# Two banks of one PSUM tile treated as one: the waits between them declared unneeded in a fused attention and gated-product kernel

## The chip, the core and the metric

The kernel runs on one core of a Trainium2 chip. A core has a matrix engine (PE, with weight loads listed apart as PEld), a vector engine (DVE), a scalar engine (ACT), a general engine (POOL), and a sequencer (SP) that issues the transfers which 16 DMA engines carry out. The engines run on their own and wait for each other by semaphores. The matrix engine writes its results into PSUM, which has eight banks; ACT and DVE read them from there.

The metric is the device time of one execution in microseconds (us). A profile adds the span between the first and the last instruction of one execution, which is a little shorter than the device time.

## What is computed

A recurrent attention with a forget gate runs over 768 steps for 4 batches and 8 heads of width 48. Its result, 3072 tokens of width 384, goes through a gated product of inner width 2048.

```python
# q, k, v, f_logit: (4, 8, 768, 48)
f = 1.0 / (1.0 + np.exp(-f_logit))
for t in range(S):
    state = f[:, :, t, :, None] * state + np.einsum('bhd,bhe->bhde', k[:, :, t], v[:, :, t])
    y[:, :, t] = np.einsum('bhd,bhde->bhe', q[:, :, t], state)
x = y.transpose(0, 2, 1, 3).reshape(B * S, H * D)   # (3072, 384)
h = x @ w_in                                        # (3072, 2048)
g = h * np.cos(h)
out = g @ w_out                                     # (3072, 384)
```

The kernel works in chunks of 128 steps. Within a chunk, scores of queries against keys are masked and multiplied with the values; across chunks a small state per head is carried (`st`, `sz` in the profile). The chunk's result `xT` has its channels on the partitions, so that the gated product can use it directly.

## The kernel before

A planner written in Python places every operation on an engine, gives it its buffers and fixes the order; the operations are then emitted in that order, and the framework adds the semaphores by looking at which tiles each instruction reads and writes.

PSUM is handed out from four tiles that are two banks wide each. A large operation takes a whole tile; a small one takes one bank, that is, one half of a tile.

```python
def halves(name, n, width, dt, space=None, zero=None):
    ts = [(space or cpool).tile([128, 2 * width], dt, name=f"{name}_{i}") for i in range(n)]
    # ... (cut)

base = halves("ps", 4, 512, F32, space=ppool)          # 4 tiles of two banks
phS = Banks(base, 2, [0, 2, 4], "ph")                   # h = x @ w_in: whole tiles
scS = Banks(base, 2, [4, 6, 2], "sc")                   # scores and others: whole tiles
p1S = Banks(base, 1, [7, 6, 5, 4, 3, 2, 1, 0], "p1")    # one bank

# class Banks (cut)
def ap(self, s):
    t, w = self.base["tiles"][s // 2], self.base["width"]
    return t if self.size == 2 else t[:, (s % 2) * w:(s % 2) * w + w]
```

The gated product works on units of 128 or 256 tokens. First h into two banks (line 728), its cosine on ACT (line 735), and the product of the two on DVE (line 738), which gives the tile gT:

```python
nc.tensor.matmul(ph.ap[:, g * T:(g + 1) * T], lhsT=w_in_bf[...], rhs=x[:, m, :], ...)   # L728
# ACT: co = sin(h + pi/2)                                                                # L735
# DVE: gT = h * co                                                                       # L738
```

Then the output product, 16 matmuls for each 128 tokens into one bank, planned as four operations of four so that other work can stand between them, and a copy out of PSUM (on ACT or DVE) that is then stored:

```python
for i in range(T // C):
    po, ot = Val(p1S), Val(otS)
    for s in range(4):
        def g2(e, i=i, s=s, po=po):
            for j in range(4 * s, 4 * s + 4):
                nc.tensor.matmul(po.ap[:, 0:d_model], lhsT=gT.ap[:, j, i * C:(i + 1) * C],
                                 rhs=w_out_bf[:, j, :], start=(j == 0), stop=(j == KF - 1))   # L748
        P.op("o", {"PE": mm(384, 4)}, g2, reads=[gT, w_out_v[s]], writes=[po], prio=pr)
    P.op("ot", {"ACT": act(384), "DVE": dve(384)}, ...)                                       # L751
    # the store of ot, L759 and L762 (cut)
```

The attention of one chunk, as far as its lines are named further on:

```python
# qk: queries and keys times decay, on POOL or DVE          L540, L632
# vb, vz: values cast to bf16, on ACT, POOL or DVE           L403
# qkt: queries and keys turned, by PE (L559, L654) and a copy out of PSUM (L427), or by DMA (L645)
# sc: scores, PE                                             L572, L667
# am: scores times mask, DVE                                 L578, L670
# ps: the chunk's own part of the state, PE                  L592, L680
# st: that part + the state before, DVE                      L497
# sz: st times decay, POOL (in the first chunk DVE)          L504
# px: the chunk's result, PE                                 L705 (first chunks: L611, L618)
# xT: its copy out of PSUM, ACT or DVE                       L427
# cum: sums of the gate's logarithm, PE                      L465 to L477
```

Of the kernel before, what the change touches and what calls it, by code (L numbers as in the profile page):

```python
# [15 lines left out]
class Slots:  # L16


    def __init__(self, aps, name):
        self.aps, self.name = aps, name  # L20
        self.free_at = [0.0] * len(aps)
        self.held = [False] * len(aps)
        self.last, self.now = [[] for _ in aps], [[] for _ in aps]
# [87 lines left out]

class Op:
    __slots__ = ("seq", "eng", "fn", "prio", "table", "deps", "vals", "alloc", "start", "end",
                 "lat", "waiting", "after", "grp", "dma", "name", "prior", "cost")


class Plan:
# [126 lines left out]
        return order  # L244


GROUPS = [(2, 2), (2, 2), (2, 2), (2, 2), (2, 2), (2, 2)]
UNITS = [128, 128] + [256] * 11
DUAL = [0, 2, 4]
# [29 lines left out]
       "DVE", 759: "ACT", 775: "ACT", 776: "ACT", 778: "DVE", 782: "ACT", 803: "ACT", 809: "ACT"}  # L279


def build(nc, cpool, ppool, q, k, v, f_logit, moe_w_in, moe_w_out, out):
    B, H, S, D = 4, 8, 768, 48
    C = 128
    NCH = S // C
# [45 lines left out]
    def halves(name, n, width, dt, space=None, zero=None):  # L331
        ts = [(space or cpool).tile([128, 2 * width], dt, name=f"{name}_{i}") for i in range(n)]
        if zero is not None and nc is not None:
            for t in ts:
                zero(t)
        return {"held": [False] * 2 * n, "free": [0.0] * 2 * n, "last": [[] for _ in range(2 * n)],
                "now": [[] for _ in range(2 * n)], "tiles": ts, "width": width}
# [25 lines left out]
    base = halves("ps", 4, 512, F32, space=ppool)  # L363
# [1 line left out]
    scS = Banks(base, 2, [4, 6, 2], "sc")  # L365
    p1S = Banks(base, 1, [7, 6, 5, 4, 3, 2, 1, 0], "p1")

    P = Plan()
    HB = lambda a: a.rearrange("p (h d) -> p h d", d=D)

    def act(n, src="P", ptr=False):
        return 0.833 * n + (160 if src == "P" else 198) + (95 if ptr else 0) - 55

# [11 lines left out]
    def load_weights(part, i, prio):  # L385
# [6 lines left out]
        def fn(e):  # L392
            if part == 0:
                src = moe_w_in.rearrange("(km p) f -> p km f", p=128)[:, :, i * 512:(i + 1) * 512]
            else:
                src = moe_w_out.rearrange("(kf p) m -> p kf m", p=128)[:, i * 4:(i + 1) * 4, :]
            nc.sync.dma_start(out=view(), in_=src)
        P.op(f"w{part}{i}", {"SP": 420.0}, fn, writes=[stage], prio=prio, dma=2080.0)
        P.op("wc", {"POOL": 1480.0, "DVE": 920.0, "ACT": act(1536, "S")}, lambda e:
             cast(e, dst.ap, view()), reads=[stage], writes=[dst], prio=PR["wc"][4 * part + i])  # L400

    def cast(e, o, i_):
        (nc.scalar.copy if e == "ACT" else nc.vector.tensor_copy if e == "DVE" else nc.gpsimd.tensor_copy)(  # L403
            out=o, in_=i_)

    def load(t, src, b, c, n, prio, nm, eng="SP"):

        def fn(e):
# [3 lines left out]
            else:  # L412
                i_.dma_start(out=o.rearrange("p (h x) -> p h x", h=H),
                             in_=src[b, :, c * C:(c + 2) * C, :].rearrange("h (p e) d -> p h (e d)", e=2))
        P.op(nm + str(n), {eng: 430.0 if n not in DUAL else 500.0}, fn, writes=[t], prio=prio,
             dma=1000.0 if n not in DUAL else 1430.0)
# [12 lines left out]
    def decay(chunks, g, prio):  # L429
# [5 lines left out]
        for i, (b, c, n) in enumerate(chunks[:1] if dual else chunks):  # L435
            load(ft.part((lambda a: flat(a)) if dual else (lambda a, i=i: a[:, i].rearrange("p h d -> p (h d)"))),
                 f_logit, b, c, n, PR["f"][n], "f")

        first = P.op("exp", {"ACT": act(384 * m, "S")}, lambda e: nc.scalar.activation(  # L439
            out=flat(ft.ap[:, 0:m]), in_=flat(ft.ap[:, 0:m]), func=AF.Exp, scale=-1.0),  # L440
# [329 lines left out]
    n, t0, units = 0, 0, list(UNITS)  # L770
    for g, group in enumerate(GROUPS):
        at0 = n
# [23 lines left out]
@with_exitstack  # L796
def kernel(
    ctx: ExitStack,
    tc: tile.TileContext,
    q: bass.AP,  # L800
    k: bass.AP,
    v: bass.AP,
    f_logit: bass.AP,
    moe_w_in: bass.AP,
    moe_w_out: bass.AP,
    out: bass.AP,
):
    nc = tc.nc
    cpool = ctx.enter_context(tc.tile_pool(name="const", bufs=1))
    ppool = ctx.enter_context(tc.tile_pool(name="psum", bufs=1, space=bass.MemoryType.PSUM))  # L810
    with tc.manual_schedule():
        order = build(nc, cpool, ppool, q, k, v, f_logit, moe_w_in, moe_w_out, out).run()
        table = None
        for o in order:
            if o.table is not None:
                if o.table == "E" and table != "E":
                    nc.scalar.preload_act_table_set("natural_log_exp_and_others")
                table = o.table
            o.fn(o.eng)


# [28 lines left out]
```

## Time and profile before

| | |
|---|---|
| device time, median of 3 runs | 202.4 us (202.11 to 203.04) |
| span in the profile | 199.2 us |
| L748, output product | 384 matmuls, 69.7 us busy, 326 ns each |
| L728, product h | 624 matmuls, 68.5 us busy |
| L738, DVE product of h and cosine | 48, 58.1 us busy, 1220 ns each |
| L735, ACT cosine | 48, 53.3 us busy, 1115 ns each |
| L751, copy of the output | 14 on ACT, 482 ns each; 10 on DVE, 557 ns each |

In the profile, PE, DVE and the others are rows of instructions, each with its source line. An idle time in front of an instruction is put down to the releaser, the instruction whose semaphore came last. Idle time of an engine costs something only where the chain of work that ends last runs through that engine. A wait in front of an instruction can have two reasons: it needs what the other has made, or the other still uses the place into which it will write. The view does not say which of the two it is; that is read from the source.

### The profile page before, as it was taken

The page shows a single profiled execution, that of the slowest core. Times are in us where ns is not written, and L with a number is a line of the kernel's source. Part 1 is how long each engine was busy: PE and PEld are TensorE (multiplying, and loading weights), DVE is VectorE, ACT ScalarE, POOL GpSimd, SP SyncE. Part 2 cuts the span into 40 slices and gives each one's busy share as a digit, 9 for nine tenths or more (in the row PEclk, how much of TensorE's full clock was granted, in tenths as well). Part 3 has the DMA queues.
Part 4 walks back from the last instruction along what each step waited for, and adds up shares of the span by engine and source line. Part 5 has one row for each costly group of instructions (what it writes and reads, how often), then busy time and mean ns, then how long its engine had stood idle before and what let it go on. Part 6 is the DMA issues. An engine that isn't in the chain of part 4 may idle for free. (4 is left out here: it accounts for less than half of the span.)

```text
span 199.2 us, 5276 instructions
## 1 busy us (share of the span) xinstructions
PE 176.3 (89%) x2194; PEld 129.0 (65%) x2194; DVE 123.8 (62%) x152; ACT 130.7 (66%) x163; POOL 75.7 (38%) x119
## 2 busy tenths in 40 slices
PE   0477999999999988998999999998998899998883
PEld 0355898765678755767866678755776657885451
DVE  5139689838868931786991778973474694587100
ACT  3694578987668978987789658878564454572010
POOL 8337232139631108879523972127902220000000
PEclk9999999999999999999999999999999999999999
DMA  6999999999899799799999999951331210101212
GB/s 158 302 277 313 358 252 294 207 298 236 171 191 214 168 204 220 174 220 186 192 216 174 242 216 179 216 120 44 94 95 40 53 44 3 40 0 40 81 40 79
DMA packets 106264, 33.11 MB, mean 166 GB/s; under 512 B 99584, under 2 KB 104704, under 8 KB 106240
## 3 DMA queue, kind: packets, MB, share of 16 engines
q1 hardware_dynamic: 106240, 32.78, 74.9%
q8 instruction: 17, 0.28, 0.7%
q14 instruction: 7, 0.06, 0.1%
HBM read 25.17 MB, written 4.72 MB: 150 GB/s over the span
## 5 line engine op out<-in xcount | busy, mean ns | idle before, releaser
L748 PE MATMUL ps<-w_out_bf,gT 128*128 128x384 bf16 x384 | 69.7, 326 | 7.0 <-DVE ot L751 2.6
L735 ACT ACTIVATE cosh<-ps,halfpi 128x1024 bf16<-128x1024 f32 x48 | 53.3, 1115 | 23.8 <-PE ps L728 23.1
L728 PE MATMUL ps<-xT,w_in_bf 128*128 128x256 bf16 (+1 forms) x624 | 68.5, 267 | 0.4
L738 DVE TENSOR_TENSOR gT<-ps,cosh 128x1024 bf16<-128x1024 f32 x48 | 58.1, 1220 | 15.1 <-ACT cosh L735 12.8
L728 PEld LDWEIGHTS <-w_in_bf 128*128 128x128 bf16 x624 | 57.1, 99 | 8.6 <-DVE xT L427 0.5
L748 PEld LDWEIGHTS <-gT 128*128 128x128 bf16 x384 | 35.5, 97 | 31.1 <-issue 9.2
L504 POOL TENSOR_TENSOR sz<-st,b 64x192 bf16<-64x192 f32 x32 | 16.3, 510 | 31.0 <-DVE st L497 29.7
L632 POOL TENSOR_TENSOR qk<-ld,b 128x384 bf16<-128x384 f32 x18 | 18.5, 1044 | 14.4 <-ACT b L483 9.1
L670 DVE TENSOR_TENSOR am<-ps,umask 128x1024 bf16<-128x1024 f32 x18 | 21.9, 1218 | 3.1 <-PE ps L667 2.8
L751 ACT COPY ot<-ps 128x384 f32<-128x384 f32 x14 | 6.7, 482 | 18.3 <-PE ps L748 17.2
L632 POOL TENSOR_TENSOR qk<-ld,bi 128x384 bf16<-128x384 f32 x18 | 17.8, 1002 | 0.2
L403 POOL CAST vb<-ld 128x384 bf16<-128x384 f32 x13 | 6.6, 507 | 25.7 <-DMA ld<-in_v_dram 19.8
L497 DVE TENSOR_TENSOR st<-ps,sz 128x384 f32<-128x384 f32 x16 | 8.8, 552 | 8.8 <-PE ps L748 5.9
L751 DVE COPY ot<-ps 128x384 f32<-128x384 f32 x10 | 5.6, 557 | 12.8 <-PE ps L748 10.2
L483 ACT ACTIVATE b<-ps 128x776 f32<-128x776 f32 x12 | 9.8, 820 | 5.5 <-PE ps L471 2.3
L439 ACT ACTIVATE f<-f 128x768 f32<-128x768 f32 x12 | 9.7, 840 | 3.6 <-DMA f<-in_f_logit_dram 3.5
L483 ACT ACTIVATE bi<-ps 128x768 f32<-128x768 f32 x12 | 9.8, 814 | 0.0
L454 ACT ACTIVATE sp<-f 128x768 bf16<-128x768 f32 x12 | 9.5, 829 | 0.1
L427 DVE COPY qkt<-ps 128x1024 bf16<-128x1024 bf16 x8 | 5.5, 687 | 6.0 <-ACT vz L403 2.0
L559 PE MATMUL ps<-ident,qk 128*128 128x128 bf16 x48 | 5.5, 279 | 3.5 <-DVE qk L540 2.2
L578 DVE TENSOR_TENSOR am<-ps,pmask 128x1024 bf16<-128x1024 f32 x6 | 7.2, 1221 | 1.9 <-PE ps L572 1.9
L465 PE MATMUL ps<-sp,incl 128*128 128x384 bf16 x6 | 2.6, 431 | 6.3 <-ACT sp L454 6.3
(77 smaller groups left out, 182.4 us busy)
## 6 DMA issues: line engine op xcount, KB each, us to landing
f<-in_f_logit_dram SPq DMA_DIRECT2D x18, 192.0 KB, 3.7
ld<-in_v_dram SPq DMA_DIRECT2D x18, 192.0 KB, 4.0
ld<-in_k_dram SPq DMA_DIRECT2D x18, 192.0 KB, 3.8
ld<-in_q_dram SPq DMA_DIRECT2D x18, 192.0 KB, 3.6
out_dram<-ot SPq DMA_DIRECT2D x18, 192.0 KB, 1.9
gT<-in_moe_w_in_dram SPq DMA_DIRECT2D x4, 768.0 KB, 7.6
gT<-in_moe_w_out_dram SPq DMA_DIRECT2D x4, 768.0 KB, 7.4
f<-in_f_logit_dram SPq DMA_DIRECT2D x3, 384.0 KB, 6.0
```

The lines of the kernel that those rows point to most:

```text
L439: first = P.op("exp", {"ACT": act(384 * m, "S")}, lambda e: nc.scalar.activation(out=flat(ft.ap[:, 0:m]), in_=flat(ft.ap[:, 0:m]), func=AF ...
L454: nc.scalar.activation(out=o, in_=i_, func=AF.Ln, bias=1.0)
L483: nc.scalar.activation(out=out_.ap[:, 0:m, :], in_=i, func=AF.Exp, scale=s)
L497: P.op("st", {"DVE": dve(384)}, lambda e: nc.vector.tensor_add(out=like(st.ap, pv()), in0=pv(), in1=like(S_in.ap, pv())), reads=[ps[0], S_ ...
L504: eng().tensor_mul(out=like(S_out.ap, pv())[s, ..., r, :], in0=srcap()[s, ..., r, :], in1=d[..., None].broadcast_to(list(d.shape) + [D]))
L632: P.op("qk", {"POOL": 1020.0}, lambda e, j=j, src=src, dec=dec: E(e).tensor_mul(out=qkv()[:, j, :, 0:D], in0=HB(src.ap), in1=HB(dec.ap[:, ...
L670: P.op("am", {"DVE": dve(1024)}, lambda e: nc.vector.tensor_mul(out=am.ap.rearrange("p r a n -> p (r a) n"), in0=sc.ap.rearrange("p (a n) ...
L728: nc.tensor.matmul(ph.ap[:, g * T:(g + 1) * T], lhsT=w_in_bf[:, f0 // 512, m, f0 % 512:f0 % 512 + 128], rhs=x[:, m, :], start=(g % (G // 2 ...
L735: nc.scalar.activation(out=co.ap, in_=ph.ap, func=AF.Sin, bias=halfpi),
L738: P.op("g", {"DVE": dve(1024)}, lambda e, ph=ph, co=co, gv=gv: nc.vector.tensor_mul(out=gv.ap, in0=ph.ap.rearrange("p (g t) -> p g t", t=T ...
L748: nc.tensor.matmul(po.ap[:, 0:d_model], lhsT=gT.ap[:, j, i * C:(i + 1) * C], rhs=w_out_bf[:, j, :], start=(j == 0), stop=(j == KF - 1))
L751: P.op("ot", {"ACT": act(384), "DVE": dve(384)}, lambda e, po=po, ot=ot: (nc.scalar.copy if e == "ACT" else nc.vector.tensor_copy)(out=ot. ...
```

## The change

The framework tracks who reads and who writes each PSUM tile. In the kernel before, the two banks of a tile are one thing to it: an instruction that writes into one bank waits for the readers of the other, and a reader of one bank waits for the writers of the other, though no byte is shared. The change records every emitted instruction and tells the framework, for each operation that uses PSUM, that it has no dependence on operations of other engines in the other bank of its tile. Dependences that the plan itself knows of (what an operation reads, and who used its buffers before) are kept. Order and instructions are those of before, and so are the places in PSUM.

```diff
+def apart(tc, o, base):
+    banks = set()
+    for v in o.vals:
+        if getattr(v.pool, "base", None) is base:
+            banks.update(range(v.slot, v.slot + v.pool.size))
+    others = [b ^ 1 for b in sorted(banks) if b ^ 1 not in banks]
+    keep = [i for d in list(o.deps) + o.prior for i in d.made]
+    for b in others:
+        for e in ("PE", "ACT", "DVE", "POOL"):
+            if e != o.eng:
+                for i in o.made:
+                    tc.declare_no_dep(i, group=f"bank{b}{e}", keep=keep, reason="other PSUM bank")
+    if banks and len(others) == len(banks):
+        for b in banks:
+            for i in o.made:
+                tc.add_to_no_dep_group(f"bank{b}{o.eng}", i)
 ...
-        order = build(nc, cpool, ppool, q, k, v, f_logit, moe_w_in, moe_w_out, out).run()
+        rec = Recorded(nc)
+        P = build(nc, cpool, ppool, q, k, v, f_logit, moe_w_in, moe_w_out, out, rec)
+        order = P.run()
         ...
+            del rec.made[:]
             o.fn(o.eng)
+            o.made = list(rec.made)
+            apart(tc, o, P.banks)
```

Cut here: the classes `Recorder` and `Recorded`, which pass each call on to the engine and keep the instruction that it returns, and a field `made` for it. An operation that uses a whole tile (both banks) declares nothing and joins no group.

More of the change, by code (lines that the diff above doesn't have):

```diff
@@ L113 @@
     __slots__ = ("seq", "eng", "fn", "prio", "table", "deps", "vals", "alloc", "start", "end",
-                 "lat", "waiting", "after", "grp", "dma", "name", "prior", "cost")
+                 "lat", "waiting", "after", "grp", "dma", "name", "prior", "cost", "made")
 class Plan:
@@ L244, in run, with __init__, __getattr__, call @@
         return order
+class Recorder:
+    def __init__(self, engine, to):
+        self._engine, self._to = engine, to
+    def __getattr__(self, name):
+        f = getattr(self._engine, name)
+        def call(*a, **k):
+            r = f(*a, **k)
+            self._to.append(r.ins)
+            return r
+        return call
+class Recorded:
+    def __init__(self, nc):
+        self.made = []
+        for e in ("tensor", "vector", "scalar", "gpsimd", "sync"):
+            setattr(self, e, Recorder(getattr(nc, e), self.made))
+def apart(tc, o, base):
[14 more added lines that the diff above has]
+                tc.add_to_no_dep_group(f"bank{b}{o.eng}", i)
 GROUPS = [(2, 2), (2, 2), (2, 2), (2, 2), (2, 2), (2, 2)]
@@ L279, with build @@
        "DVE", 759: "ACT", 775: "ACT", 776: "ACT", 778: "DVE", 782: "ACT", 803: "ACT", 809: "ACT"}
-def build(nc, cpool, ppool, q, k, v, f_logit, moe_w_in, moe_w_out, out):
+def build(nc, cpool, ppool, q, k, v, f_logit, moe_w_in, moe_w_out, out, rec=None):
     B, H, S, D = 4, 8, 768, 48
@@ L366, in build @@
     p1S = Banks(base, 1, [7, 6, 5, 4, 3, 2, 1, 0], "p1")
-    P = Plan()
+    P, nc = Plan(), rec or nc
+    P.banks = base
     HB = lambda a: a.rearrange("p (h d) -> p h d", d=D)
```

## The prediction

> **What bounds the kernel now.** I read the page's first two parts, then the waits of the matrix engine (PE) by stage, then the timeline around its gaps.
>
> ```profile
> PE 176.3 (89%) x2194; PEld 129.0 (65%) x2194; DVE 123.8 (62%) x152; ACT 130.7 (66%) x163; POOL 75.7 (38%) x119
> ...
> PE   0477999999999988998999999998998899998883
> ...
> DMA  6999999999899799799999999951331210101212
> ```
>
> The first line is busy time and share by engine, the other two are busy tenths in slices of 5 us. PE works nearly without a break from 20 us to 195 us, so what takes idle time out of PE can shorten the kernel. The DMA line shows a second thing that is full: the 16 DMA engines, until about 127 us (slice 25). After that DMA hardly matters. By stage (the table of windows) the DMA share is 0.96 from 50 to 97.6 us and 0.86 from 97.6 to 150 us, and 0.13 after.
>
> Next, who makes PE idle. Columns: engine, line, releaser, total us, times, longest. First 50 to 97.6 us, then 97.6 us to the end.
>
> ```profile
> PE ps L748 <- DVE ot L751: 1.3, 2, 0.6
> PE ps L680 <- ACT xT L427: 0.6, 1, 0.6
> ```
>
> ```profile
> PE ps L748 <- DVE ot L751: 1.3, 2, 0.6
> PE ps L748 <- DVE xT L427: 1.1, 2, 0.6
> PE ps L748 <- DVE qkt L427: 0.8, 1, 0.8
> PE ps L748 <- ACT ot L751: 0.8, 2, 0.6
> PE ps L748 <- ACT xT L427: 0.6, 1, 0.6
> PE ps L748 <- DVE st L497: 0.4, 1, 0.4
> ```
>
> In the second stretch all of PE's idle time of note, 5.0 us in nine waits, stands before the output product (L748). A matmul there needs only the gated tile, the weights and a bank of PSUM. None of the named releasers makes any of these: ot, xT, qkt and st are copies or sums that read PSUM, so PE waits until someone has finished reading. The timeline shows what they read:
>
> ```profile
> 179.59 1.46 PE L748 MATMUL ps<-w_out_bf,gT 128*128 128x384 bf16 x8
> ...
> 181.09 0.56 DVE L751 COPY ot<-ps 128x384 f32<-128x384 f32 x1 [0.24 <-PE ps L748]
> ...
> 181.70 5.36 PE L748 MATMUL ps<-w_out_bf,gT 128*128 128x384 bf16 x32 [0.65 <-DVE ot L751]
> ```
>
> Eight matmuls: the last four of one accumulation and the first four of the next, which stands in the other bank of the same two-bank tile. The copy needs only the first four, which end at 180.40 us (179.59 + 3 x 0.162 + 0.326, pitch and length from below), yet it starts at 181.09, after all eight. Then PE waits for the copy, 0.56 us and the hand-over, before it goes on in the bank that the copy never touches. It is a wait in each direction, and neither carries data.
>
> **What the Trainium skill says.** "PSUM — Partial Sum Buffer", section "PSUM bank collisions raise a hardware error", reports that two engines on different banks run clean, so the order that is given up here protects nothing. The trace agrees as far as it goes: the copy of ot takes 0.56 us at 181.09 with PE idle and 0.56 us at 183.85 in the midst of matmuls into another tile. "Perfetto Trace Analysis", section "Identifying the Most-Contended Engine", warns that pipelined matmuls make busy time a poor measure. That matters for the sum: 32 matmuls of 326 ns take 5.36 us, so their pitch is (5.36 - 0.33)/31 = 0.162 us, and a gap in a row of them costs its idle time plus the lost overlap, 0.326 - 0.162 = 0.16 us. Section "Identifying Dependency Chains" of the same page says that an instruction waiting on several engines may get an extra semaphore instruction. One such on PE shows in the trace, 51 ns long.
>
> **The change part by part.** *Removed.* In the built program 27 matmuls lose a wait for ACT or DVE or get it later, and 22 reads of PSUM by ACT and DVE wait for an earlier matmul than before. Matching each lost wait with the gap in front of it, after 97.6 us: 109.87 us 0.39, 130.45 us 0.48, 137.39 us 0.65, 151.05 us 0.83, 156.48 us 0.57, 162.38 us 0.24, 181.70 us 0.65, 187.71 us 0.65, 193.63 us 0.57. The sum is 5.03 us: every one of the nine goes. Six of them stand between two matmuls of L748 (all but those at 109.87, 130.45 and 162.38), so 6 x 0.16 = 0.98 us of overlap comes back: 6.0 us.
>
> *Before 97.6 us* the lost waits measure 0.28, 0.18, 0.32 (all at 51 to 56 us), 0.65 (71.61 us) and 0.65 (78.67 us), with the overlap some 2.9 us, and part of 0.63 at 94.64 us. I choose to count almost none, because the loads do not come sooner:
>
> ```profile
> 91.31 0.51 ACT L403 CAST vb<-ld 128x384 bf16<-128x384 f32 x1 [1.47 <-DMA ld<-in_v_dram]
> ...
> 92.10 2.12 ACT L735 ACTIVATE cosh<-ps,halfpi 128x1024 bf16<-128x1024 f32 x2
> ...
> 93.25 2.36 DVE L738 TENSOR_TENSOR gT<-ps,cosh 128x1024 bf16<-128x1024 f32 x2 [1.41 <-ACT cosh L735]
> ...
> 94.11 0.49 ACT L427 CAST xT<-ps 128x384 bf16<-128x384 f32 x1
> ...
> 94.64 0.33 PE L680 MATMUL ps<-vb,qk 128*128 128x96 bf16 x4 [0.63 <-ACT xT L427]
> ```
>
> ACT sits at a cast until its load lands at 91.29 us, in a stream that fills the DMA engines, and then works without a gap through a cast, a copy and two cosines to the xT copy that ends at 94.60. L680 no longer has to wait for that copy, but the L728 matmul after it reads that xT, and may start at 94.64 instead of 94.81. DVE follows the same load: its row of five operations from 93.25 ends at 97.49, and frees the tile for the L728 matmul that now starts at 97.60. So PE can be ahead by no more than about 0.06 us at 97.6, however much it gained before. I add 0.1 us.
>
> *Added.* Nine semaphore instructions, three on ACT and six on DVE, none on PE; at 51 ns, under 0.5 us spread over two engines with a third of their time free. *Moved.* Order and instructions stay.
>
> *What stays behind it.* A gain is real only if the next wait does not catch it. After 97.6 us PE would be ahead by 0.6 us at 110, 1.2 at 131, 2.0 at 138, 3.0 at 151, 3.8 at 156, 4.1 at 162 and 6 at the end (running sums with the overlap). The surviving waits there hang on PE's own earlier work (cosine on L728, product on cosine) and move with it. Those that hang on loads have room: key and query blocks turned by DMA are there 2.0 us early at 101, 2.1 at 112, 3.5 at 125, 5.7 at 132 and 3.0 at 145.5 (landing against first use). The tightest I found is L705 at 154.6, whose state sz was done 0.83 us earlier; but the DVE sum under it waited for an xT copy that it no longer waits for, so it moves up by as much.
>
> Sum: 202.4 - 6.0 - 0.1 = 196.3 us, 3.0% less.
>
> **The rivals.** (1) *The early gain survives too.* If loads land earlier because ACT frees their buffers earlier, 2.9 us more: 193.3 us. Against it stands the full DMA line. (2) *A new wait takes the place of the old.* If the sz chain at 154.6 does not move, PE is held to 0.8 us ahead there in place of 3, which leaves 202.4 - 6.1 + 2.2 = 198.5 us. For it: POOL waits 29.7 us in all for st, more than any other pair. (3) *Banks of one tile disturb each other,* and reads beside matmuls get slower: 24 ot copies at, say, 10% of 0.5 us are 1.2 us, and mostly beside PE. (4) *Nothing*, because PE was not what ended last: the chain of the last 49 us is nearly all PE, with these copies as its only interruptions, so I hardly believe it.
>
> **Range and chances.** The size rests on nine waits that can be pointed at, on the part of the kernel where DMA is idle or has room; the doubt is in the catching up. I take 194.5 to 198.2 us: below lies the better part of rival 1, above lies most of rival 2. The line of 2% is 198.35 us. Faster by over 2%: 0.92; within 2%: 0.07; slower: 0.01.
>
> **What would show it.** PE's waits before L748 after 97.6 us should fall from 5.0 us to under 0.5, with ot copies beside running matmuls and still 0.56 us (DVE) and 0.48 (ACT). The part after 150 us should shrink by some 4.3 us (its six waits and their overlap). Before 97 us, PE's idle time should not vanish but gather in front of L728, L667 or L474, released by ACT and DVE work that itself waits for loads. PE busy stays near 176 us. I am wrong if the idle time comes back as waits of L705 for sz or of L728 for gT, if copies or matmuls get longer, or if the moment when the cast at 91.31 us starts moves by more than half a microsecond.

## The result, and the profile after

The changed kernel takes 195.57 us (median of 4 runs, 194.95 to 196.81) against 202.58 us (the three runs of the table ahead and a fourth): a ratio of 0.966 with a 95% interval of 0.961 to 0.972. The prediction was 196.3 us. The profiled span went from 199.2 to 193.2 us; that is 6.0 us where the medians differ by 7.0, because the profile of before is of a faster run (200.93 us).

First the page after. Every call now passes through one recording helper, so all instructions stand under its line, L257, and one goes by the tiles' names: `ps<-w_out_bf,gT` is the former L748.

```profile
PE 174.9 (91%) x2194; PEld 129.1 (67%) x2194; DVE 123.0 (64%) x152; ACT 129.4 (67%) x163; POOL 75.3 (39%) x119
...
PE   0386799999999999699999999999999999999992
...
DMA  6999999899999988898999999999332301100222
...
L257 PE MATMUL ps<-w_out_bf,gT 128*128 128x384 bf16 x384 | 68.3, 326 | 0.4 <-DVE w_out_bf L257 0.4
...
L257 ACT COPY ot<-ps 128x384 f32<-128x384 f32 x14 | 6.7, 487 | 13.9 <-PE ps L257 13.8
...
L257 DVE COPY ot<-ps 128x384 f32<-128x384 f32 x10 | 5.5, 552 | 8.7 <-PE ps L257 5.2
```

The work is the same; the span is shorter. After slice 17, which ends at about 82 us, the PE row is all nines up to the last slice. In front of the output product 0.4 us of idle time is left (it was 7.0), and that one waits for weights. A matmul still takes 326 ns and the copies 487 and 552 ns (482 and 557 before), so no slowing of either is seen when one bank is read while another is written.

The same place in the timeline as the prediction showed, some 180 us into the kernel:

```profile
175.95 13.81 PE L257 MATMUL ps<-w_out_bf,gT 128*128 128x384 bf16 x84
...
177.12 0.55 DVE L257 COPY ot<-ps 128x384 f32<-128x384 f32 x1
177.59 1.21 DVE L257 TENSOR_TENSOR gT<-ps,cosh 128x1024 bf16<-128x1024 f32 x1
...
179.40 0.56 DVE L257 COPY ot<-ps 128x384 f32<-128x384 f32 x1 [0.59 <-PE ps L257]
182.00 0.56 DVE L257 COPY ot<-ps 128x384 f32<-128x384 f32 x1 [2.04 <-PE ps L257]
```

84 matmuls in one row of 13.81 us, with the copies beside them. The rows of 8, 32, 32 and 12 that the copies had cut it into are gone.

Who PE waits for, 97.6 us to the end: the view has no row at all; the six rows that summed to 5.0 us have gone. From 50 to 97.6 us it has these (releaser, total us, times, longest):

```profile
PE ps L257 <- ACT sp L257: 1.9, 2, 1.6
PE ps L257 <- ACT xT L257: 0.4, 1, 0.4
PE ps L257 <- ACT qkt L257: 0.3, 1, 0.3
PE ps L257 <- POOL sz L257: 0.3, 1, 0.3
```

These are mostly new names, with nearly the old total (2.9 us against 3.1). PE comes to them sooner and waits longer. What stands under two of them is seen in the timeline:

```profile
80.66 1.56 ACT L257 ACTIVATE sp<-f 128x768 bf16<-128x768 f32 x2
81.54 0.32 PE L257 MATMUL ps<-sp,umask 128*128 128x384 bf16 x1 [1.63 <-ACT sp L257]
```

```profile
91.91 0.51 ACT L257 CAST vb<-ld 128x384 bf16<-128x384 f32 x1 [2.04 <-DMA ld<-in_v_dram]
...
94.46 0.33 PE L257 MATMUL ps<-vb,qk 128*128 128x96 bf16 x4
94.70 0.49 ACT L257 CAST xT<-ps 128x384 bf16<-128x384 f32 x1
...
95.24 0.49 PE L257 MATMUL ps<-xT,w_in_bf 128*128 128x256 bf16 x3 [0.45 <-ACT xT L257]
```

The logarithm sp follows an exponential that began at 79.91 us, when its gate load had landed at 79.81. And the cast that waits for a v load now waits 2.04 us where it waited 1.47. The state product (`ps<-vb,qk`) no longer waits for the xT copy and runs at 94.46, but the product on that xT still must.

To compare kernels I use one fixed matmul, the 1139th of 2194, which began at 97.60 us in the trace of before; call it **the mark**. Times are from start to start. The kernels below "after" are those of the experiments.

| kernel | ratio to before (95%) | cast of v begins | mark | mark after cast | mark to last matmul |
|---|---|---|---|---|---|
| before | 1 | 91.31 | 97.60 | 6.29 | 97.82 |
| after | 0.966 (0.961 to 0.972) | 91.91 | 98.14 | 6.23 | 91.29 |
| after, second time | 0.964 (0.962 to 0.966) | 91.08 | 97.31 | 6.24 | 91.32 |
| early only | 0.999 (0.996 to 1.002) | 91.21 | 97.44 | 6.23 | 97.86 |
| late only | 0.967 (0.963 to 0.970) | 90.31 | 96.61 | 6.30 | 91.29 |
| matmuls only | 0.969 (0.965 to 0.973) | 92.13 | 98.36 | 6.24 | 91.79 |
| readers only | 0.974 (0.970 to 0.977) | 92.37 | 98.66 | 6.29 | 92.75 |
| light loads, before | 0.994 (0.991 to 0.996) | 89.43 | 96.49 | 7.07 | 97.82 |
| light loads, after | 0.946 (0.940 to 0.953) | 86.10 | 93.17 | 7.07 | 91.30 |
| other sequence, before | 0.998 (0.996 to 1.000) | 91.75 | 98.82 | 7.07 | 97.82 |
| other sequence, after | 0.952 (0.947 to 0.958) | 87.26 | 94.33 | 7.07 | 91.51 |
| its gate part, after | 0.965 (0.961 to 0.968) | 91.42 | 97.65 | 6.23 | 91.29 |
| its v part, after | 0.960 (0.957 to 0.962) | 88.97 | 96.04 | 7.07 | 91.29 |

Ratios are of several runs each, times in us from one profile each, and a single profile can lie off: that of "other sequence, before" is of its slowest run (202.15 us; the median is 200.36).

### The profile page after: what moved, and what is told of

It reads as the page before. It is cut to its first block, busy times and chain, and to the rows that moved or that the text cites. A ratio compares the mean times of both kernels' runs of the same rounds, so it can differ in the third digit from the quotient of the medians.

```text
span 193.2 us, 5285 instructions
## 1 busy us (share of the span) xinstructions
PE 174.9 (91%) x2194; PEld 129.1 (67%) x2194; DVE 123.0 (64%) x152; ACT 129.4 (67%) x163; POOL 75.3 (39%) x119
## 4 chain that ended last, share of the span: by engine, by line
PE 66%; DMA 8%; SPq 6%; DVE 5%; ACT 5%; issue 4%; POOL 4%; POOLq 0%; ACTq 0%; DVEq 0%
PE ps L257 66%; DMA ld<-in_v_dram 6%; SPq L257 6%; POOL qk L257 3%; DMA ld<-in_q_dram 2%; DVE am L257 2%; ACT cosh L257 1%; DVE w_out_bf L257 1%; ACT f L257 1%; ACT L865 1%; DVE gT L257 1%; DVE qk L257 1%; POOL sz L257 1%; DVE vb L257 0%; ACT xT L257 0%
## 5 line engine op out<-in xcount | busy, mean ns | idle before, releaser
L257 PE MATMUL ps<-xT,w_in_bf 128*128 128x256 bf16 (+1 forms) x624 | 68.8, 268 | 0.7 <-ACT xT L257 0.4
L257 DVE TENSOR_TENSOR gT<-ps,cosh 128x1024 bf16<-128x1024 f32 x48 | 58.0, 1219 | 17.9 <-ACT cosh L257 16.0
L257 ACT ACTIVATE cosh<-ps,halfpi 128x1024 bf16<-128x1024 f32 x48 | 53.0, 1114 | 23.5 <-PE ps L257 23.2
L257 PE MATMUL ps<-w_out_bf,gT 128*128 128x384 bf16 x384 | 68.3, 326 | 0.4 <-DVE w_out_bf L257 0.4
L257 PEld LDWEIGHTS <-w_in_bf 128*128 128x128 bf16 x624 | 57.4, 100 | 9.0 <-DVE xT L257 0.5
L257 PEld LDWEIGHTS <-gT 128*128 128x128 bf16 x384 | 35.3, 98 | 22.9 <-issue 0.5
L257 POOL TENSOR_TENSOR qk<-ld,b 128x384 bf16<-128x384 f32 x22 | 23.2, 1065 | 24.4 <-DMA ld<-in_q_dram 11.6
L257 POOL TENSOR_TENSOR sz<-st,b 64x192 bf16<-64x192 f32 x32 | 16.1, 502 | 24.8 <-DVE st L257 23.1
L257 DVE TENSOR_TENSOR am<-ps,umask 128x1024 bf16<-128x1024 f32 x18 | 21.8, 1218 | 5.6 <-PE ps L257 5.5
L257 POOL TENSOR_TENSOR qk<-ld,bi 128x384 bf16<-128x384 f32 x22 | 22.5, 1035 | 0.2
L257 POOL CAST vb<-ld 128x384 bf16<-128x384 f32 x13 | 6.6, 505 | 27.5 <-DMA ld<-in_v_dram 21.0
L257 PEld LDWEIGHTS <-qk 128*128 128x128 bf16 (+1 forms) x212 | 12.7, 109 | 6.5 <-issue 2.4
L257 ACT COPY ot<-ps 128x384 f32<-128x384 f32 x14 | 6.7, 487 | 13.9 <-PE ps L257 13.8
L257 ACT ACTIVATE f<-f 128x768 f32<-128x768 f32 x12 | 9.7, 840 | 5.4 <-DMA f<-in_f_logit_dram 5.4
L257 PE MATMUL ps<-ident,qk 128*128 128x128 bf16 x104 | 9.9, 247 | 3.6 <-DVE qk L257 2.2
L257 ACT ACTIVATE b<-ps 128x776 f32<-128x776 f32 x12 | 9.9, 823 | 3.6 <-PE ps L257 2.7
L257 DVE TENSOR_TENSOR st<-ps,sz 128x384 f32<-128x384 f32 x16 | 8.8, 551 | 5.5 <-PE ps L257 4.1
L257 PEld LDWEIGHTS <-qkt 48*128 48x128 bf16 (+2 forms) x260 | 7.4, 109 | 6.1 <-issue 2.8
L257 DVE COPY ot<-ps 128x384 f32<-128x384 f32 x10 | 5.5, 552 | 8.7 <-PE ps L257 5.2
L257 PE MATMUL ps<-qkt 48*128 48x128 bf16 (+1 forms) x240 | 10.0, 238 | 1.1 <-ACT qkt L257 1.0
L257 PE MATMUL ps<-sp,incl 128*128 128x384 bf16 (+1 forms) x12 | 4.0, 379 | 6.4 <-ACT sp L257 6.4
L257 ACT ACTIVATE bi<-ps 128x768 f32<-128x768 f32 x12 | 9.8, 818 | 0.0
```

The lines of the kernel that those rows point to most:

```text
L257: r = f(*a, **k)
```

## Experiments

### Where the gain is made: one half of the kernel at a time

```diff
+            products += len(o.made) if o.eng == "PE" else 0
-            apart(tc, o, P.banks)
+            if products < 1138:        # early only; late only has >= 1138
+                apart(tc, o, P.banks)
```

Early only: 

> The waits between banks are given up only for operations emitted before the 1138th matmul (97.6 us in the profile of before); after it everything is as before. Theory (early gain is swallowed by loads that land no sooner): 202.5 us, within 0.7 us of before; the matrix engine is ahead by about 1.3 us at 71 us and by nothing at 95 us, where it waits for the xT copy on ACT. Rival (early gains survive to the end): 2.9 us less, 199.7 us.

Late only: 

> The waits are given up only from the 1138th matmul on. Theory (all of the gain is made after 97.6 us): the same time as with all of them given up, 195.6 us, within 0.7 us. Rival (the parts before matter for some 2 us by letting later work be ready): 197.5 us or more.

Measured: 0.999 and 0.967. The late half alone has the whole gain; the early half has none that can be measured. It does make PE faster for a while: in the early-only kernel the matmul that waited for a copy until 71.61 us before now begins at 70.61 (I had said 1.3 us ahead), and the next such one begins at 76.86 instead of 78.67. At the mark 0.16 us of these 1.81 is left, 0.10 of it because the v load came that much sooner. PE's waits from 50 to 97.6 us tell where the rest went:

```profile
PE ps L257 <- ACT sp L257: 1.2, 1, 1.2
PE ps L257 <- POOL sz L257: 0.4, 1, 0.4
PE ps L257 <- ACT qkt L257: 0.3, 1, 0.3
PE ps L257 <- ACT xT L257: 0.2, 1, 0.2
```

They are the names of the changed kernel again, not those of before. Most of the lead is lost earlier than I had expected: after the wait for sp, at 80.96 us, PE is 0.50 us ahead; not at 95 us, where the wait for the xT copy takes 0.2. The rival, that 2.9 us survive to the end, is out.

### Which of the two directions costs: matmuls or readers

```diff
-            if e != o.eng:
+            if e != o.eng and o.eng == "PE":    # matmuls only; readers only has != "PE"
```

Matmuls only: 

> Only matmuls stop waiting for readers of the other bank; ACT and DVE reads of PSUM still wait for matmuls in the other bank. Theory (the gain is the matrix engine's waits, the late copies are beside the path): 195.8 us, no wait of the matrix engine after 97.6 us, the copies of ot still start after the fourth matmul of the next group. Rival (readers must come sooner too, else states and xT arrive late and new waits appear): 198 us or more.

Readers only: 

> Only ACT and DVE reads of PSUM stop waiting for matmuls in the other bank; matmuls still wait for those reads. Theory (a copy of 0.56 us on DVE or 0.48 us on ACT then runs beside the four matmuls of 0.65 us, and the matrix engine is held 0.16 or 0.08 us in place of 0.81 at most of the nine places; the one at 162.4 us, whose copy had its data late, stays with 0.4): 5.6 of 6.5 us gained, 197.0 us, idle time of the matrix engine before L748 under 1 us after 97.6 us. Rival (only the matrix engine's own wait counts): 202.5 us.

Measured: 0.969 and 0.974. From the mark to the last matmul 6.0 of 6.5 us are gained by the one and 5.1 by the other. So it is not the sum of two costs: the two waits stand in a row, the reader for four matmuls and the next matmul for the reader, and to break either opens it. In the matmuls-only kernel the copy is as late as before, and PE runs on beside it:

```profile
176.82 3.41 PE L257 MATMUL ps<-w_out_bf,gT 128*128 128x384 bf16 x20
...
178.16 0.56 DVE L257 COPY ot<-ps 128x384 f32<-128x384 f32 x1 [0.24 <-PE ps L257]
```

The late copies are not quite free: the 0.5 us that this kernel lacks is lost at four other starts, each held 0.07 to 0.19 us by a copy of ot or a DVE product (am, gT), too short to show as a wait.

In the readers-only kernel the copy no longer waits for the four matmuls. About half of it runs beside them, and PE waits for the rest.

```profile
178.39 0.55 DVE L257 COPY ot<-ps 128x384 f32<-128x384 f32 x1
...
178.99 1.30 PE L257 MATMUL ps<-w_out_bf,gT 128*128 128x384 bf16 x7 [0.32 <-DVE ot L257]
```

My 0.16 us for this place was too small: the data is there at about 178.02, but DVE is still in the product before it, so the copy starts at 178.39. In all, PE idles 0.7 us after the mark where I had said under 1.

### What swallows the early gain: loads

Light loads leave out a part of the work: from the seventh chunk on, q, k, v and the gate are fetched for four of eight heads, and the rest of each buffer keeps what an earlier chunk left. The engines' instructions are all there, only the transfers shrink.

```diff
+            if n >= 6:
+                i_.dma_start(out=HB(o)[:, 0:4], in_=src[b, 0:4, c * C:(c + 1) * C, :].rearrange("h p d -> p h d"))
```

On the kernel before: 

> The kernel before, but the loads of q, k, v and the gate fetch only four of eight heads from the seventh chunk on (the other half of each buffer keeps what an earlier chunk left; the output is not the reference's): about half of the bytes after 35 us. Theory (before 97.6 us the kernel is held in part by loads): some waits at 91 to 97 us go, 1 to 2 us less than before: 201.0 us. Rival (loads do not hold anything): 202.5 us.

On the changed kernel: 

> The changed kernel with the same halved loads. Theory (the early gain of 2.9 us was there and the full load stream swallowed it): with room in the stream it comes back, 8.5 to 9.5 us less than the light kernel before: 192.0 us. Rival (the early gain is swallowed by a chain of ACT or DVE work, not by loads): 6.5 to 7 us less than the light kernel before: 194.3 us.

Measured: 199.67 and 190.35 us, 9.3 us apart. With the full loads the two were 6.8 us apart (0.0338 x 202.58). The missing 2.5 us come back when the loads have room, so they were there and were swallowed by loads, not by a chain of ACT, DVE or POOL work, which is untouched here. After the mark, light and full kernels take the same time (97.82 and 97.82; 91.30 and 91.29): all of the difference lies ahead of it.

### The same with all bytes: the sequence of the load queue

The landing times showed that loads stand in the queue in an order that does not follow their need. Ahead of the v load used 0.02 us after landing, the trace of before has gate loads used 12 to 17 us and even 51 us after theirs. This kernel moves them behind it, and puts the two gate loads that ACT waits for at 79 us ahead of the two halves of a store. Every other engine keeps its order.

```diff
-        order = P.run()
+        order = other_queue(P.run())
+    # queue from the gate loads of chunks 14, 15 on (f: gate, st: store)
+    # was: st f15 f14 f23 f22 st v15 k13 st q13 k18 f18 q18 f17 v12 f19 f16 k19 q19 k15 q15 st
+    # now: f15 f14 st v15 k13 st q13 k18 q18 v12 f18 f17 f19 f16 k19 q19 k15 q15 st st ... f20 f23 f22
```

On the changed kernel: 

> The changed kernel with another sequence in the load queue between 72 and 110 us: the gate loads for the chunks used at 79 us go ahead of two stores, the v load that ACT waits for at 91 us goes ahead of gate loads that are not used before 103 us, and two gate loads used at 131 us go behind those. Bytes and all other engines' orders stay. Theory (loads that came late swallowed the early gain): 1.5 to 2.9 us less than the changed kernel: 193.5 us, the ACT cast of v starting some 4 us earlier. Rival (other chains hold it): 195.6 us.

On the kernel before: 

> The kernel before with that same sequence of the load queue. Theory (in the kernel before the matrix engine had little to gain from earlier loads, only its waits at 82 to 98 us): 0.5 to 1 us less, 201.8 us. Rival (the sequence by itself is worth as much as in the changed kernel): 2 us less, 200.5 us.

Measured: 0.952 and 0.998. On the changed kernel the sequence is worth 2.4 to 2.8 us (0.952 against 0.964 or 0.966), on the kernel before 0.5 us. Neither change does alone what both do. The cast of v begins at 87.26 us, and not for a landing any more: it lines up behind a cosine. PE's waits from 50 to 97.6 us:

```profile
PE ps L257 <- ACT qkt L257: 0.3, 1, 0.3
PE ps L257 <- ACT sp L257: 0.2, 1, 0.2
```

This is the fastest kernel here that loads every byte, 191.72 us where the kernel before took 200.88 us in the same comparison.

### Which load holds

The two parts of that sequence, one at a time, beside the changed kernel.

```diff
-    new = [f15, f14, st, v15, k13, ...]
+    new = [f15, f14, st, then all others as planned]   # gate part
+    new = [st, f15, f14, v15, k13, ...]                # v part
```

The changed kernel again: 

> The changed kernel once more, as the yardstick for the two kernels beside it: 0.966 of the kernel before.

The gate part: 

> The changed kernel with only the first part of the other load sequence: the two gate loads that ACT waits for at 79.9 us go ahead of the two halves of one store, all else stays. Theory (two holds in a row, and the later one decides): the matrix engine waits less at 81.5 us but is held by the v load at 95 us as before: within 0.5 us of the changed kernel. Rival (the gate loads were the hold that mattered): 1.5 us or more less.

The v part: 

> The changed kernel with only the second part: the v load that ACT waits for at 91.9 us goes ahead of gate loads not yet needed, the gate loads for 79.9 us stay where they were. Theory: the hold at 81.5 us stays, what is lost after it comes back; 1.0 to 1.8 us less than the changed kernel, between it and the kernel with both parts. Rival (the v load does not matter alone): within 0.5 us of the changed kernel.

Measured: 0.964, 0.965 and 0.960. The gate part alone brings nothing: in its profile PE passes the wait for sp at 79.61 instead of 81.28 us and loses the lead again before the mark. Where it loses it, its waits and POOL's timeline show:

```profile
PE ps L257 <- POOL sz L257: 1.5, 2, 1.3
PE ps L257 <- ACT xT L257: 0.6, 1, 0.6
```

```profile
86.28 1.00 POOL L257 TENSOR_TENSOR qk<-ld,b 128x384 bf16<-128x384 f32 x1 [3.70 <-DMA ld<-in_q_dram]
```

So there is a third load, which I had not counted: POOL stands 3.70 us for a q load (q13 in the list, landed at 86.15), its sz comes late by that, and PE waits 1.3 us for sz at 89.33, ahead of the xT copy at 94.75. The v part moves that q load too: it lands at 82.88 there, and the wait for sz is gone. The v part brings 0.9 us by the ratio and 1.3 us at the mark of the two profiles, at the low end of what I expected or just under it; how much of that is the v load's and how much the q load's, no run separates. Both together bring 2.4 us by the ratio (from another comparison) and 3.0 at the mark, which is more than the sum of the parts. The holds stand one behind the other, at 81.5, 89 and 95 us; the later ones decide, and with them gone the earliest one shows.

## Why the prediction was right, step by step

**The nine waits.** All nine went, as said. From the mark to the last matmul I had 6.0 us; the traces say 97.82 - 91.29 = 6.53. My two sums did not agree: the running sums counted an overlap at all nine places, and 4.1 at 162 us with three more gaps of 0.81, 0.81 and 0.73 makes 6.45; the total counted it at six. The running sums were the better ones (measured 4.2 at 162 us). The six between two matmuls of L748 were summed right: 0.81, 1.00, 0.73, 0.81, 0.81 and 0.73 are 4.89 us, against 3.92 of idle time and 0.98 of lost overlap. Mis-sized were the three others, for which I took the idle time alone (1.11 us): the stretches around them shrank by 0.46, 0.64 and 0.30, or 1.40 us, since after a small matmul too the start is lost that would have overlapped. The rest, some 0.24 us, is what I left out: a sum of the gate that had waited on a late DVE row at 134.8 us (0.15), and two starts held by less than 0.1 each.

**The early gain.** I said that PE could be ahead by about 0.06 us at the mark. Measured from the cast that waits for the v load, the mark comes 6.29 us later before and 6.23 after: 0.06. Wherever the cast waits for that load the table has the same two numbers: 6.23 or 6.24 with the early matmuls freed, 6.29 or 6.30 where they still wait (before, late only, readers only). It is the DVE row that holds there, as said: in the changed kernel the mark is released by the DVE product that ends 0.05 us ahead of it, while before that product ended 0.11 us ahead and PE's row ran through. But the v load is only the last of the holds. I argued from it alone; most of the early lead is lost before it, behind a gate load (1.3 of 1.8 us in the early-only kernel, at 80.96 us) and a q load. The bound was right, its account of where the lead goes was incomplete. The v load itself landed 0.6 us later in the first profile of the changed kernel and 0.2 earlier in the second, so these profiles show no effect of the change on it; I had named half a microsecond as a sign that I was wrong, and that limit was tighter than the loads are steady.

**What stays behind it.** Nothing caught the late gain. The chain I held for the tightest, the state at 154.6 us, moved as I thought: the sum under it began at 149.30 instead of 152.05, and sz was done at 151.01 instead of 153.75. Rival 2 is out by that, rival 3 by the 326, 487 and 552 ns (before 326, 482 and 557).

**The loads as the reason** were an argument in the prediction. The light loads and the other sequence show it: of the 2.9 us that rival 1 counted, 2.5 come back with light loads and 2.4 to 2.8 with the other sequence. The gain is real, and needs loads that come in time.

**After 150 us** I said some 4.3 us; PE's lead grew from 1.61 us ahead of its wait at 151 us to 5.98 at the end, 4.4.

## What to carry to other kernels

When a matmul waits for a copy, ask from the source whether it needs what the copy makes or only the place, and then whether it is really the same bank: a framework may guard a whole tile where only one bank of it is in use. A gap in a row of pipelined matmuls costs its idle time and an overlap besides, and it can be counted as gain only up to the next thing that does not move with it; here that was loads, and they had taken back all that was won ahead of them. A change that frees an engine and a change that brings its loads in time can be worth more together than apart (here 4.8% against 3.4 to 3.6% and 0.2%), so look at the load queue again after the engine has become faster.

## What I had not expected

The sequence alone of 24 transfers among 133 decided over more than 2 us, in a stretch where the DMA engines were full and no byte was saved: gate loads that nobody read for 51 us had stood ahead of a load that was read 0.02 us after it landed. And the part after the mark is steadier than the loads: the cast moved between 90.31 and 92.37 us from one kernel to another with the same queue, while the time from the mark to the last matmul agreed within 0.05 us wherever the late half was the same, with one exception (91.51 with the other sequence, where one matmul of h starts 0.23 us late, behind a copy of ot on ACT).
